# A fused attention and feed-forward kernel: weight operands formed earlier, combinations kept in PSUM, and activation sums moved to GpSimd

## The chip, the cores and the metric

One core of a Trainium2 chip runs the whole kernel in one launch. The metric is the device time of one execution in microseconds, a median over runs. Engine names are short: PE is TensorE, DVE is VectorE, ACT is ScalarE, POOL is GpSimd, SP is SyncE, which issues the DMAs.

## The reference

Three parts follow one another. The input of each is the output of the one before.

```python
def _attn_ref(q, k, v, w1, b1, w2):           # (4, 8, 576, 64)
    scores = scale * np.matmul(q, k.transpose(0, 1, 3, 2))
    ...
    scores = scores + bias.transpose(2, 0, 1)[None, :, :, :]
    ...
def _moe_ref(x, w_in, w_out, a, b):           # 2304 tokens, 512 -> 2048 -> 512
    h = x @ w_in
    P = a[0] + a[1] * h + a[2] * h2 + a[3] * h3
    Q = 1.0 + np.abs(b[0]) * np.abs(h) + np.abs(b[1]) * h2
    g = P / (Q + 1e-06)
    return (g @ w_out).astype(np.float32)
def _moe2_ref(x, w1, w2, w3, w_out):          # 512 -> 768 -> 512
    h = np.maximum(np.maximum(x @ w1, x @ w2), x @ w3)
    return (h @ w_out).astype(np.float32)
```

## The kernel before

Float32 products are made from operands split in a high and a low part (type fp32r), with three matmuls for each product: high by high, high by low, low by high. So every operand needs a cast for its high part (ACT) and a subtraction for its low part (mostly POOL). The weights arrive as 64-bit numbers; a shift on ACT (L605), another on DVE (L606) and a join on DVE (L611) make 32-bit ones of them.

**Attention** fills the span to about 343 us, and **the feed-forward part** follows to about 760. It takes the tokens in five blocks (0 to 4) of 512, 512, 256, 512 and 512. A block has sixteen steps, one for each 128 of the 2048 hidden columns. `ffn_tick(n)` writes one step: twelve matmuls for `ph` (the hidden columns of step n), twelve for `y` (the second matmul of step n-2), and between them the rational function g: `rat_poly`, `rat_inv`, `rat_newton` on ACT and DVE, and `rat_split`, whose high part is an ACT cast (L554) and whose low part is POOL's `gs` (L555). Each `g` tile comes from a ring of pools ("big").

**The third part (moe2)** runs from about 757 to the end. It works on three super blocks of 768 tokens (`sbk` 0 to 2). In each there are nine units `un` = 3 jp + w, where w is one of the three weight matrices and jp one of three pairs of 128-column groups. A unit is a two by two block product made with seven products instead of eight (Strassen's method in Winograd's form). `product` is six matmuls of 384 columns into one PSUM bank `pr`; `combine` adds the seven into the four results; `result` takes the maximum over w into `m`. The combination `c` goes to SBUF (L763) and the maximum L766 runs one or two products later, kept in a list by `after`. With w = 2 the finished `m` is split into `h2` (L753 on ACT, L751 on POOL). The steps of the w_out matmul (`o`, L828), two after each product, fill the next jp.

Seven products need seven weight operands (four sums of blocks among them) and seven activation operands (again with four sums). Before the change the 64-bit weights of moe2 are made 32-bit in blocks 1 and 3 and written to memory (`mn_d`, `mon_d`). They are read back in the last block and in super block 0 by `operand_stages`, one unit after the other: load, four sums on DVE (L643 to L646), casts on ACT (L655), low parts on POOL (L662), and a store to `ms_d` (L663). Super blocks 1 and 2 load the finished parts from `ms_d` (L689). The activation sums are four DVE operations of 768 columns (L718 to L721), with casts on ACT (L709) and low parts on POOL (L710, L711), in steps 9 to 15 of block 4 and, for the later super blocks, from product (7, 0) to (8, 6) of the super block before (`YN`).

PSUM has two `wide` tiles of two banks and four single banks. The `o` sums use both wide tiles and two of the four banks while they run, so that a product then has two banks left, and the bank of product n is written again by product n+2.

The order on SP, PE, DVE and POOL is that of the program text (`MANF`); ACT runs in program order too. `moe_product` sets the order in moe2: the matmuls, `combine`, the `o` steps, the delayed work of `product_tick`, and then one or two stages of the weight queue (`op_next`) and one of the y queue.

## Time and profile before

| | us |
|---|---|
| runs | 1055.9, 1059.98, 1060.53 |
| median of the three | 1059.98 |
| profiled execution, device time | 1058.46 |
| profiled execution, span | 1056.7 |
| PE busy in the span | 1009.1 |
| DVE, ACT, POOL busy | 786.5, 633.2, 478.8 |

Times in the trace count from the start of the span. An engine's busy time over a stretch is what its instructions cover; the rows further down give it by stretch, and PE's granted clock beside it (1.00 is 2.4 GHz, half of it 1.2 GHz). In the timeline a bracket such as [0.90 <-POOL gs L555] is the idle time of the engine ahead of the row, and what ended it. The PE rows overlap slightly, since matmuls are pipelined.

### The profile page before, as it was taken

What the parts mean: (1) busy time and instruction counts of PE and PEld (TensorE: products, weight loads), DVE (VectorE), ACT (ScalarE), POOL (GpSimd) and SP (SyncE); (2) the same over time, 40 slices, a digit from 0 to 9 for tenths busy, and PEclk for the clock granted to TensorE, in tenths of its full rate; (3) what the DMA queues carried; (4) which work ended last, traced back from release to release, by engine and by line L of the source; (5) the groups of instructions that cost most, each with busy time, mean ns of one, the idle gap of its engine ahead of it and who ended that gap; (6) DMA issues with size and microseconds to landing.
All of it is one profiled execution on the core that took longest, in us unless ns stands there. A gap on an engine that the chain in (4) does not pass through costs nothing. (4 is left out here: it accounts for less than half of the span.)

```text
span 1056.7 us, 17453 instructions
## 1 busy us (share of the span) xinstructions
PE 1009.1 (96%) x6050; PEld 824.1 (78%) x6050; DVE 786.5 (74%) x1549; ACT 633.2 (60%) x1258; POOL 478.8 (45%) x634
## 2 busy tenths in 40 slices
PE   6899999999998999999999999999899999999997
PEld 2368777777776678788899888788798989988996
DVE  8876587877675789889888899888797655565543
ACT  8867676777677778777778777778542121131111
POOL 4035677768686345422324223338677351152111
PEclk9999999999999999999999999999999999999999
DMA  7977666565544143044420344243186548744711
GB/s 256 333 249 210 235 217 197 174 207 194 172 143 148 54 145 100 1 150 130 149 80 2 100 140 150 100 165 114 69 310 254 195 148 283 246 160 161 270 49 60
DMA packets 69127, 172.22 MB, mean 163 GB/s; under 512 B 7088, under 2 KB 22960, under 8 KB 69040
## 3 DMA queue, kind: packets, MB, share of 16 engines
q1 hardware_dynamic: 69040, 171.12, 48.3%
q8 instruction: 47, 0.77, 0.3%
q14 instruction: 40, 0.33, 0.1%
HBM read 118.27 MB, written 52.82 MB: 162 GB/s over the span
## 5 line engine op out<-in xcount | busy, mean ns | idle before, releaser
L779 PE MATMUL pr<-yo,ws 128*128 128x384 f32 x945 | 221.9, 339 | 8.6 <-DVE m L760 5.2
L507 PE MATMUL y<-gs,wwo 128*128 128x512 f32 (+1 forms) x940 | 215.0, 375 | 5.1 <-POOL gs L555 4.1
L507 PE MATMUL ph<-xs,wwi 128*128 128x512 f32 (+1 forms) x930 | 207.0, 370 | 1.6 <-POOL xs L499 1.4
L555 POOL TENSOR_TENSOR gs<-g,gs 128x512 fp32r<-128x512 f32 (+1 forms) x80 | 95.5, 1193 | 226.8 <-ACT gs L554 156.4
L507 PEld LDWEIGHTS y<-gs,wwo 128*128 128x128 f32 x940 | 165.0, 189 | 41.9 <-POOL gs L555 7.0
L779 PEld LDWEIGHTS pr<-yo,ws 128*128 128x128 f32 x945 | 172.6, 189 | 23.0 <-DVE m L760 6.3
L507 PEld LDWEIGHTS ph<-xs,wwi 128*128 128x128 f32 x930 | 162.2, 188 | 35.4 <-POOL xs L499 3.6
L266 ACT ACTIVATE e<-e,st 128x576 f32<-128x576 f32 x144 | 110.8, 771 | 69.1 <-DVE st L260 46.5
L260 DVE CUSTOM_DVE_ANT_0 e<-s,bias 128x576 f32<-128x576 f32 x144 | 103.6, 752 | 17.4 <-PE s L235 11.1
L828 PE MATMUL o<-wmo,h 128*128 128x512 f32 x324 | 100.1, 397 | 2.8 <-DVE ot L813 2.0
L794 ACT COPY u<-pr 128x384 f32<-128x384 f32 x27 | 13.0, 481 | 146.0 <-PE pr L779 96.0
L751 POOL TENSOR_TENSOR h<-m,h 128x384 fp32r<-128x384 f32 x36 | 36.7, 1040 | 134.7 <-ACT h L753 109.8
L528 ACT ACTIVATE s<-ph,keep 128x512 f32<-128x512 f32 (+1 forms) x80 | 49.3, 617 | 64.2 <-PE ph L507 64.0
L235 PE MATMUL s<-k,qs 128*128 128x288 f32 x512 | 85.0, 308 | 1.9 <-ACT bo L197 1.0
L307 PEld LDWEIGHTS tp<-ident,e 128*128 128x128 f32 x564 | 60.4, 141 | 32.1 <-issue 15.9
L349 PE MATMUL av<-at,v 128*64 128x320 f32 (+3 forms) x576 | 77.4, 393 | 7.2 <-ACT at L1030 5.6
L307 PE MATMUL tp<-ident,e 128*128 128x128 f32 x564 | 78.6, 280 | 0.6 <-DVE att L328 0.6
L235 PEld LDWEIGHTS s<-k,qs 128*128 128x128 f32 x512 | 70.8, 190 | 4.1 <-DVE st L260 1.9
L530 DVE SCALAR_TENSOR_TENSOR g<-g,keep,s 128x512 f32<-128x512 f32 (+1 forms) x80 | 55.3, 691 | 21.6 <-ACT g L529 20.2
L542 DVE SCALAR_TENSOR_TENSOR g<-g,keep,s 128x512 f32<-128x512 f32 (+1 forms) x80 | 55.5, 694 | 16.8 <-ACT s L536 12.0
L828 PEld LDWEIGHTS o<-wmo,h 128*128 128x128 f32 x324 | 58.7, 189 | 6.7 <-DVE ot L813 2.1
L779 PE MATMUL pr<-yl,ws 128*128 128x384 f32 x189 | 63.4, 335 | 0.0
(140 smaller groups left out, 1842.0 us busy)
## 6 DMA issues: line engine op xcount, KB each, us to landing
ws<-ms_d SPq DMA_DIRECT2D x54, 512.0 KB, 4.1
ms_d<-ws SPq DMA_DIRECT2D x27, 512.0 KB, 3.1
bias_d<-bo SPq DMA_DIRECT2D x36, 288.0 KB, 6.6
kr<-in_k SPq DMA_DIRECT2D x16, 576.0 KB, 3.9
qr<-in_q SPq DMA_DIRECT2D x16, 576.0 KB, 4.9
bias<-bias_d SPq DMA_DIRECT2D x16, 576.0 KB, 5.8
nr<-in_m SPq DMA_DIRECT2D x18, 512.0 KB, 3.6
wrwin<-in_wi SPq DMA_DIRECT2D x16, 512.0 KB, 4.7
```

What stands on the lines that cost most here:

```text
L235: pe.matmul(pt[:, x, :HS], lhsT=qs[:, u, t * P:(t + 1) * P], rhs=ks[u][:, w, x * HS:(x + 1) * HS], start=w == 0, stop=w == 1,)
L260: dve.tensor_tensor_reduce(out=dst, in0=src, in1=bs, op0=ALU.add, op1=ALU.min, scale=-0.125, scalar=3.0e38, accum_out=st[:, u:u + 1],)
L266: act.activation(et[:, u], et[:, u], AF.Exp, bias=st[:, u:u + 1], scale=-1.0, accum_out=st[:, 2 + u:3 + u])
L307: pe.transpose(tp[:, j * P:(j + 1) * P], flat[:, 640 * u + j * P:640 * u + (j + 1) * P], ident)
L349: pe.matmul(po[r, :n], lhsT=l, rhs=m, start=j == 0, stop=j == 4, skip_group_check=True)
L507: pe.matmul(po, lhsT=wpart(key, a, k), rhs=rhs, start=first and i == 0, stop=last and i == 2)
L528: act.activation(s, ph, AF.Abs, scale=B0)
L530: dve.scalar_tensor_tensor(q, q, B1, s, ALU.mult, ALU.add)
L542: dve.scalar_tensor_tensor(u, u, A0, s, ALU.add, ALU.mult)
L555: pool.tensor_tensor(t[1], u, f32(t[0]), ALU.subtract)
L779: pe.matmul(pt, lhsT=w[:, a, ch * P:ch * P + P], rhs=ys[c][ch], start=ch == 0 and i == 0, stop=ch == 1 and i == 2,)
L828: pe.matmul(po, lhsT=h[:, a, (tt % 3) * P:(tt % 3 + 1) * P], rhs=mo_t[j][:, c], start=j == 0 and i == 0, stop=j == NF2 - 1 and i == 2,)
```

## The change

- **Weight units.** The round trip through `mn_d` and `mon_d` is gone. `unit_stages` loads two raw 64-bit pieces, makes them 32-bit, forms the four sums on POOL, and splits all parts; a table `PLAN` says which unit is made in which block and at which steps. Units 2, 3, 4 are made in block 1, unit 5 in block 2, units 6, 7, 8 in block 3, units 0 and 1 in block 4. The last two stay in SBUF. The others pass through one tile with two halves (`wring`) to `ms_d`, and super block 0 loads them back like the later super blocks do; the first three of these loads stand in steps 13 to 15 of block 4 (`WPN`).
- **w_out tiles.** `out_stages` makes the six tiles 32-bit and splits them during the first products of super block 0, one stage after each product.
- **g tiles.** All but the first three use two halves of one tile (`gring`).
- **Activation sums.** They stand on POOL, in another form of the same products (t3, t2, t1, t4), in steps 5 to 12 of block 4 and from product (6, 2) to (8, 5).
- **Combinations.** `result` writes the combination back into the PSUM bank and takes the maximum from there at once. The delayed list and the `c` tiles go. The low part of `h2` is issued with its cast.
- **Last unit.** The last `o` steps are set up at product 20 (`OE`); the order of PE's instructions at the end is the same.

```diff
-KN = {... 'YL': 7, 'YS': 9, ... 'OPA': 2, 'OPR': 2, 'WR': 7, ... 'YN': [(7, 0), (7, 3), (7, 6), (8, 3), (8, 4), (8, 5), (8, 6)], ...}
+KN = {... 'YL': 4, ... 'YN': [(6, 2), (6, 4), (6, 6), (7, 1), (7, 3), (7, 5), (8, 1), (8, 3), (8, 4), (8, 5)], ... 'YSN': {5: 2, 6: 2, 7: 1, 8: 1, 9: 1, 10: 1, 11: 1, 12: 1}, 'PLAN': [(2, 1, [0, 2, 3, 4, 5, 6, 7, 8]), (3, 1, [4, 6, 7, 8, 9, 10, 11, 12]), ... (5, 2, [1, 3, 5, 6, 8, 10, 12, 14]), ... (0, 4, [0, 2, 3, 4, 5, 6, 7, 8]), (1, 4, [6, 8, 9, 10, 11, 12, 13, 14])], 'WPN': {13: 1, 14: 1, 15: 1}, ...}
...
+            bt = gring[0][:, len(gring) % 2]
+            gring.append(None)
...
-            sp.dma_start(dst, f32(t))
-
-        return [load, rebias, join]
...
         def sums():
-            r = box["r"]
-            box["s"] = t = raw(f"os{un}", [P, 2, 512], F32)
...
-            seng.tensor_tensor(s1, a21, a22, ALU.add)
-            seng.tensor_tensor(s3, a11, a21, ALU.subtract)
...
+            pool.tensor_tensor(s1, a21, a22, ALU.add)
+            pool.tensor_tensor(s3, a11, a21, ALU.subtract)
+            pool.tensor_tensor(s2, s1, a11, ALU.subtract)
+            pool.tensor_tensor(s4, a12, s2, ALU.subtract)
...
+                t = wring[0][:, g % 2, :, :n]
+            box[g] = t
             act.copy(t[:, 0], source(g))
...
+            lambda: (ld0(), ld1()), lambda: (re0(), jo0()), lambda: (re1(), jo1()), lambda: (sums(), hi(0)),
+            lambda: (lo(0), hi(1)), lambda: (lo(1), hi(2)), lambda: (lo(2), hi(3)), lambda: lo(3),
...
+        return [load, rebias, lambda: (join(), hi()), lo]
...
     def y_stages(sbk):
         b11, b12, b21, b22 = (yr[sbk, h, t] for h in range(2) for t in range(2))
-        tt = (dve if KN["YD"] else pool).tensor_tensor
+        tt = pool.tensor_tensor
...
+        def t3():
+            tt(b12, b22, b12, ALU.subtract)
+
+        def t2():
+            for i, x in enumerate(pieces("t2")):
+                tt(x, b12[:, i], b11[:, i], ALU.add)
...
-    def result(sbk, un, jj, th, a_, b_, op, lag):
+    def result(sbk, un, jj, th, pt, a_, b_, op):
...
-        c_ = sb.tile([P, 512], F32, tag="xs", name=f"c{sbk}_{un}_{jj}{th}", bufs=KN['NXS'])[:, :TH]
-        dve.tensor_tensor(c_, a_, b_, op)
-
-        def more():
-            dve.tensor_tensor(m, m, c_, ALU.max)
-            if w == 2:
-                after(1, lambda: h2_make(sbk, 2 * jp + jj, th))
-
-        after(lag, more)
+        dve.tensor_tensor(pt, a_, b_, op)
+        dve.tensor_tensor(m, m, pt, ALU.max)
+        if w == 2:
+            h2_make(sbk, 2 * jp + jj, th)
...
+        for st in plan.pop((n // NF, n % NF), []):
+            st()
...
         if sbk == 0:
-            for _ in range(2 if n in (0, 3) else 1):
-                op_next()
+            op_next()
```

Where instructions now stand shows at three places. First DVE, in super block 0 between unit 2 and unit 3 (`pr0_2_4` is the bank of super block 0, unit 2, product 4; `os` are weight sums, `nno` a w_out tile). Before:

```order
L763 TENSOR_TENSOR c0_2_01_8893<-pr0_2_2_8886,u40_2_8878 128x384
L766 TENSOR_TENSOR m0_0_8597<-m0_0_8597,c0_2_10_8864 128x384
L766 TENSOR_TENSOR m0_0_8597<-m0_0_8597,c0_2_11_8880 128x384
L766 TENSOR_TENSOR m0_0_8597<-m0_0_8597,c0_2_01_8893 128x384
L643 TENSOR_TENSOR os6_8912<-or6_8797 128x256
L644 TENSOR_TENSOR os6_8912<-or6_8797 128x256
L645 TENSOR_TENSOR os6_8912<-os6_8912,or6_8797 128x256
L646 TENSOR_TENSOR os6_8912<-or6_8797,os6_8912 128x256
L760 TENSOR_TENSOR m0_3_8905<-pr0_3_1_8919,u10_3_8906 128x384
```

And now, on the same engine at the same place:

```order
L782 TENSOR_TENSOR pr0_2_4_8817<-pr0_2_4_8817,u30_2_8797 128x384
L783 TENSOR_TENSOR m0_0_8558<-m0_0_8558,pr0_2_4_8817 128x384
L615 SCALAR_TENSOR_TENSOR nno4_8831<-nro4_8747 128x512
L782 TENSOR_TENSOR pr0_2_2_8835<-pr0_2_2_8835,u40_2_8824 128x384
L783 TENSOR_TENSOR m0_0_8558<-m0_0_8558,pr0_2_2_8835 128x384
L610 TENSOR_SCALAR nro5_8799<-nro5_8799 128x512
L780 TENSOR_TENSOR m0_3_8857<-pr0_3_1_8862,u10_3_8858 128x384
```

Three maxima and four sums stood ahead of the `m` of unit 3; one shift of a w_out tile stands there now, and each maximum follows its combination.

Second DVE again, in the last unit (8) of super block 0, at the passage to super block 1 (`yr` are the activations, `u` partial results). Before:

```order
L800 TENSOR_TENSOR u30_8_9463<-pr0_8_6_9454,u20_8_9449 128x384
L721 TENSOR_TENSOR yr1_01_9239<-yr1_11_9243,yr1_00_9237 128x768
L763 TENSOR_TENSOR c0_8_10_9484<-u30_8_9463,pr0_8_3_9475 128x384
L804 TENSOR_TENSOR u40_8_9500<-pr0_8_4_9493,u20_8_9449 128x384
L763 TENSOR_TENSOR c0_8_11_9502<-pr0_8_4_9493,u30_8_9463 128x384
L763 TENSOR_TENSOR c0_8_01_9519<-pr0_8_2_9510,u40_8_9500 128x384
L766 TENSOR_TENSOR m0_6_9230<-m0_6_9230,c0_8_10_9484 128x384
L766 TENSOR_TENSOR m0_6_9230<-m0_6_9230,c0_8_11_9502 128x384
L766 TENSOR_TENSOR m0_6_9230<-m0_6_9230,c0_8_01_9519 128x384
L760 TENSOR_TENSOR m1_0_9537<-pr1_0_1_9544,u11_0_9538 128x384
```

And now:

```order
L815 TENSOR_TENSOR u30_8_9374<-pr0_8_6_9365,u20_8_9361 128x384
L782 TENSOR_TENSOR pr0_8_3_9382<-u30_8_9374,pr0_8_3_9382 128x384
L783 TENSOR_TENSOR m0_6_9132<-m0_6_9132,pr0_8_3_9382 128x384
L819 TENSOR_TENSOR u40_8_9410<-pr0_8_4_9403,u20_8_9361 128x384
L782 TENSOR_TENSOR pr0_8_4_9403<-pr0_8_4_9403,u30_8_9374 128x384
L783 TENSOR_TENSOR m0_6_9132<-m0_6_9132,pr0_8_4_9403 128x384
L782 TENSOR_TENSOR pr0_8_2_9424<-pr0_8_2_9424,u40_8_9410 128x384
L783 TENSOR_TENSOR m0_6_9132<-m0_6_9132,pr0_8_2_9424 128x384
L780 TENSOR_TENSOR m1_0_9448<-pr1_0_1_9451,u11_0_9449 128x384
```

The y sum L721 is gone from DVE, and the three maxima have moved up to their combinations.

Third POOL, at steps 5 and 6 of block 4 (`gs4_1_1` is the low part of hidden group 1 in block 4, `wg` a kept weight part, `yo` and `yl` low parts of the activations). Before:

```order
L555 TENSOR_TENSOR gs4_1_1_8040<-g4_1_7986,gs4_1_0_8039 128x512
L662 TENSOR_TENSOR ws0_0_1_8006<-os0_7909,ws0_0_1_8006 128x512
L662 TENSOR_TENSOR ws0_0_2_8052<-or0_7907,ws0_0_2_8052 128x256
L555 TENSOR_TENSOR gs4_2_1_8090<-g4_2_8034,gs4_2_0_8089 128x512
L662 TENSOR_TENSOR ws0_0_3_8056<-os0_7909,ws0_0_3_8056 128x512
L555 TENSOR_TENSOR gs4_3_1_8147<-g4_3_8084,gs4_3_0_8146 128x512
```

And now:

```order
L562 TENSOR_TENSOR gs4_1_1_8018<-gring_4861,gs4_1_0_8017 128x512
L729 TENSOR_TENSOR yr0_01_7933<-yr0_11_7937,yr0_01_7933 128x768
L733 TENSOR_TENSOR yt_8029<-yr0_01_7933,yr0_00_7931 128x384 x2
L655 TENSOR_TENSOR wg0_0_7985<-nn0_0_7884,wg0_0_7985 128x512
L562 TENSOR_TENSOR gs4_2_1_8067<-gring_4861,gs4_2_0_8066 128x512
L737 TENSOR_TENSOR yt_8029<-yr0_11_7937,yt_8029 128x384 x2
L708 TENSOR_TENSOR yo0_0_8079<-yr0_00_7931,yo0_0_8079 128x384
L709 TENSOR_TENSOR yl0_0_8080<-yr0_00_7931,yo0_0_8079 128x384
L655 TENSOR_TENSOR wg0_1_8034<-ns0_7980,wg0_1_8034 128x512
L562 TENSOR_TENSOR gs4_3_1_8123<-gring_4861,gs4_3_0_8122 128x512
```

Between two `gs` there now stand four instructions, with the activation sums among them, where one or two low parts stood.

## Rows read from the trace of the kernel before

**Rows 1.** The page, busy time (share of the span) and instructions of each engine.

```profile
PE 1009.1 (96%) x6050; PEld 824.1 (78%) x6050; DVE 786.5 (74%) x1549; ACT 633.2 (60%) x1258; POOL 478.8 (45%) x634
```

**Rows 2.** Stretches: length, busy PE, PEld, DVE, ACT, POOL, clock, DMA share, GB/s.

```profile
437.00:526.00 89.00, 88.74 (x385) 71.72 (x384) 77.79 (x120) 65.45 (x115) 24.67 (x21) 1.00 0.37 120
526.00:575.00 49.00, 48.49 (x384) 47.13 (x383) 43.24 (x99) 39.42 (x102) 16.71 (x20) 1.00 0.18 58
663.00:741.00 78.00, 77.61 (x335) 62.35 (x334) 65.82 (x98) 59.91 (x102) 41.11 (x35) 1.00 0.36 125
741.00:760.00 19.00, 16.35 (x62) 12.26 (x61) 15.34 (x23) 12.31 (x21) 13.07 (x12) 0.92 0.07 28
780.00:800.00 20.00, 16.08 (x83) 15.32 (x82) 19.02 (x29) 6.37 (x13) 16.30 (x13) 0.91 0.71 259
840.00:860.00 20.00, 17.67 (x93) 16.20 (x92) 13.54 (x20) 5.93 (x10) 13.34 (x13) 1.00 0.43 132
940.00:960.00 20.00, 17.67 (x94) 16.17 (x93) 12.55 (x19) 5.92 (x10) 13.37 (x12) 1.00 0.38 122
```

**Rows 3.** Timeline at 746 to 757: start, duration, instruction, [idle before <-releaser].

```profile
746.78 2.90 PE L507 MATMUL ph<-xs,wwi 128*128 128x512 f32 x12
...
750.99 2.83 PE L507 MATMUL y<-gs,wwo 128*128 128x512 f32 x11 [0.90 <-POOL gs L555]
...
756.07 2.16 PE L507 MATMUL y<-gs,wwo 128*128 128x512 f32 x6 [1.26 <-POOL gs L555]
```

**Rows 4.** Timeline at 786 to 795, DVE and PE, super block 0.

```profile
786.43 3.41 DVE L766 TENSOR_TENSOR m<-m,c 128x384 f32<-128x384 f32 x3
...
793.30 1.10 DVE L646 TENSOR_TENSOR os<-or,os 128x256 f32<-128x256 f32 x1
...
794.92 0.69 PE L779 MATMUL pr<-yo,ws 128*128 128x384 f32 x1 [3.92 <-DVE m L760]
```

**Rows 5.** Timeline at 849 to 858, passage from super block 0 to 1.

```profile
849.30 1.75 DVE L721 TENSOR_TENSOR yr<-yr,yr 128x768 f32<-128x768 f32 x1 [2.33 <-POOL yl L711]
...
851.56 0.97 PE L779 MATMUL pr<-yo,ws 128*128 128x384 f32 x4 [1.68 <-DVE c L763]
...
857.37 0.79 PE L779 MATMUL pr<-yo,ws 128*128 128x384 f32 x3 [0.65 <-DVE m L760]
```

**Rows 6.** Timeline at 1037 to 1043, the last unit with two banks.

```profile
1037.79 0.87 PE L779 MATMUL pr<-yo,ws 128*128 128x384 f32 x4
...
1039.04 0.56 DVE L804 TENSOR_TENSOR u<-pr,u 128x384 f32<-128x384 f32 x1 [0.96 <-PE pr L779]
...
1039.31 0.87 PE L779 MATMUL pr<-yo,ws 128*128 128x384 f32 x4
...
1039.52 0.55 DVE L763 TENSOR_TENSOR c<-pr,u 128x384 f32<-128x384 f32 x1
...
1042.24 0.73 PE L828 MATMUL o<-wmo,h 128*128 128x512 f32 x2 [0.33 <-ACT h L753]
```

**Rows 7.** Groups by line and shape: count | busy us, mean ns | idle before, releasers.

```profile
L555 POOL TENSOR_TENSOR gs<-g,gs 128x512 fp32r<-128x512 f32 x64 | 83.6, 1307 | 196.7 <-ACT gs L554 130.8 <-issue 55.2 <-PE y L507 8.3
...
L766 DVE TENSOR_TENSOR m<-m,c 128x384 f32<-128x384 f32 x72 | 46.0, 676 | 0.0
...
L402 DVE SCALAR_TENSOR_TENSOR wnwin<-wrwin 128x512 int32<-128x512 int32 x16 | 17.2, 1074 | 0.1
L611 DVE SCALAR_TENSOR_TENSOR nn<-nr 128x512 int32<-128x512 int32 x18 | 12.4, 687 | 0.8
L555 POOL TENSOR_TENSOR gs<-g,gs 128x256 fp32r<-128x256 f32 x16 | 11.9, 741 | 30.1 <-ACT gs L554 25.6 <-issue 4.2 <-POOL xs L499 0.3
L655 ACT CAST ws<-os 128x512 fp32r<-128x512 f32 x18 | 11.2, 620 | 3.6 <-DVE os L645 2.8 <-DVE os L646 0.8
...
L643 DVE TENSOR_TENSOR os<-or 128x256 f32<-128x256 f32 x9 | 7.7, 860 | 0.0
```

**Rows 8.** The page, DMA issues: count, KB each, us to landing.

```profile
ms_d<-ws SPq DMA_DIRECT2D x27, 512.0 KB, 3.1
```

More of the change, by code (lines that the diff above doesn't have):

```diff
@@ L510, in tile_attention_moe @@
     gt, ph_t, bun = {}, {}, {}
+    gring, wring = [], []
     def ffn_h(blk, f):
@@ L524, in rat_poly @@
         s = bank(f"s{blk}_{f}")[:, :n]
-        bt = (slot if blk == 0 and f < KN["RS"] else big)(f"g{blk}_{f}", [P, 2, 512], F32)
+        if blk == 0 and f < KN["RS"]:
+            bt = slot(f"g{blk}_{f}", [P, 2, 512], F32)
+        else:
+            if not gring:
+                gring.append(big("gring", [P, 2, 2, 512]))
+            bt = gring[0][:, len(gring) % 2]
+            gring.append(None)
         q, u = bt[:, 0, :n], bt[:, 1, :n]
@@ L652, in hi @@
         def hi(g):
             n = 256 * len(PAIR[g])
-            t = slot(f"ws0_{un}_{g}", [P, 2, n], F32R)
+            if keep:
+                t = slot(f"wg{un}_{g}", [P, 2, n], F32R)
+            else:
+                if not wring:
+                    wring.append(big("wring", [P, 2, 2, 512], F32R))
+                t = wring[0][:, g % 2, :, :n]
+            box[g] = t
             act.copy(t[:, 0], source(g))
-            for i, pr in enumerate(PAIR[g]):
-                ws[0, un, pr] = t[:, :, 256 * i:256 * i + 256]
@@ L708, in y_operand @@
         last = yo[sbk, "low"][:, n % 3]
-        act.copy(t[:, :2], src)
-        pool.tensor_tensor(t[:, 2], src[:, 0], f32(t[:, 0]), ALU.subtract)
-        pool.tensor_tensor(last, src[:, 1], f32(t[:, 1]), ALU.subtract)
+        if isinstance(src, list):
+            for i in range(2):
+                act.copy(t[:, i], src[i])
+        else:
+            act.copy(t[:, :2], src)
+            src = [src[:, 0], src[:, 1]]
+        pool.tensor_tensor(t[:, 2], src[0], f32(t[:, 0]), ALU.subtract)
+        pool.tensor_tensor(last, src[1], f32(t[:, 1]), ALU.subtract)
         yo[sbk, pr] = (t[:, 0], t[:, 1]), (t[:, 2], last)
@@ L735, in product_tick @@
         clock[0] += 1
-    wq = [(sbk, un, g) for sbk in range(1, NSB) for un in range(3 * NJP) for g in range(4)]
+    kept = [un for un, blk, _ in KN["PLAN"] if blk == len(blocks) - 1]
+    wq = [(sbk, un, g) for sbk in range(NSB) for un in range(3 * NJP) if sbk or un not in kept for g in range(4)]
     def operands_next():
@@ L927, in tile_attention_moe @@
     ystq = []
[L928 to L941 removed]
+    ost = [out_stages(j) for j in range(NF2)]
+    opq = [ost[0][0]]
+    for j, st in enumerate(ost):
+        opq += [s_[0] for s_ in ost[j + 1:j + 2]] + st[1:]
     def op_next():
@@ L1096, in moe_product @@
         pt = product(sbk, un, pr)
[L1097 removed]
+        if n in (1, 3, 4, 6):
             operands_next()
@@ L1101, in moe_product @@
             osteps[0] = o_steps(sbk if jp else sbk - 1, jp - 1 if jp else NJP - 1)
-        for _ in range(KN["OR"]):
+        end = (sbk, un) == (NSB - 1, 3 * NJP - 1)
+        for _ in range(KN["OE"][n] if end else KN["OR"]):
             next(osteps[0], None)
@@ L1129, in tile_attention_moe @@
             moe_product(*m)
-        assert not opq and not wq
+        assert not opq and not wq and not plan
         for _ in range(2):
             product_tick()
-        for _ in o_steps(NSB - 1, NJP - 1):
+        for _ in osteps[0]:
             product_tick()
```

142 lines of the change are left out of this document (63 added, 79 removed).

## The prediction, made before the changed kernel ran

> **What bounds the kernel now.** I read the busy line of the page first: TensorE (PE) is busy 1009.1 of the 1056.7 us span and nothing else comes near [rows 1]. So the only gain within reach is PE time that is idle or run at the half clock, and I looked for it with the table of stretches [rows 2]. The two stretches inside the feed-forward blocks have PE busy 88.74 of 89 and 48.49 of 49 us at clock 1.00: nothing to win there, only to lose. The last block up to 741 is as full (77.61 of 78). Four places are not full. The end of the feed-forward part, 741 to 760, has 16.35 of 19 busy and a mean clock of 0.92. The stretch 780 to 800 has 16.08 of 20 at 0.91. The stretches 840 to 860 and 940 to 960 have 17.67 of 20 each.
>
> The timeline then names the cause of each. **End of the feed-forward part** [rows 3]: PE runs one block of twelve `ph` matmuls (2.90 us), then waits 0.90 us for the GpSimd (POOL) half of `gs` and, one block of twelve on, 1.26 for POOL again. With a shorter wait between them, for ACT's half, these make the 2.65 us that are idle there. **At 790** [rows 4]: VectorE (DVE) does three `m` maxima out of SBUF in 3.41 us and four weight sums, the last taking 1.10, and only then the `m` of L760 that frees a PSUM bank; PE waits 3.92 us for it. **At the super-block boundaries** [rows 5]: the y sum L721 waits 2.33 us for POOL and takes 1.75 ahead of the `c` of L763, for which PE waits 1.68; then PE waits 0.65 for the `m` of L760, which again stands behind three maxima. Together 2.33 us, which is the idle time of that stretch.
>
> **What the change removes.** At 790 no sums are left in moe2, and the maxima no longer come as a batch in front of L760. I count the 3.92 us of waiting in full, and 1.6 for the clock: a mean of 0.91 over 20 us is 3.6 us at half level, worth 1.8 if PE worked throughout; part of that is inside the wait. 5.5 us. At each boundary the y sum has left DVE and the maxima are spread, so 2.33 goes, twice: 4.7. At the end of the feed-forward part the y splits and the weight splits are gone from POOL behind the last `gs`, so I let two of the three waits go (2.65 less one of 1.26, because with no `ph` block left to cover it the last chain must still be waited for: 1.4) and the clock loss, 0.08 of 19, 1.5. 2.9 us. At the tail the `h` wait of 0.33 goes [rows 6], since `h2_make` no longer waits a product: 0.3. **Gains 13.4.** Bounds: 9 if only the stall at 790 and half of the rest go; 18 if the slower first matmuls behind each wait come back too (one alone took 0.97 for four where 0.87 is usual [rows 5, 6], and at half clock it is more).
>
> **What it adds in the feed-forward blocks.** PE is full there, so the question is whether `gs` comes late. Per step of 5.56 us (89/16) POOL had one `gs` of 1.307 [rows 7] and 196.7/64 = 3.07 us of idle time ahead of it, two thirds of that for ACT's half of `gs`. The change gives blocks 1 and 3 three weight units each, in place of half of the narrow work. Per unit: four POOL sums of 128x256 at 0.74 (the 256 wide `gs` [rows 7]) = 2.96, four low parts, three at 1.3 and one at 0.74 = 4.6; ACT two shifts and four casts at about 0.62 (L655 [rows 7]), one of them narrower; DVE two joins at 0.69 (L611) and two shifts, which I put at no more than the joins. In blocks 1 and 3 twelve narrowings each go and six come, so DVE gets lighter by six joins and six shifts (at most 8 us), ACT heavier by some 3, POOL by 3 x 7.6 = 23: from 24.67 to 47 us of 89, or 53%. The last block already has POOL at 41.11 of 78 (53%) with PE at 77.61 [rows 2], so that share alone is no loss. The sharp steps are those with sums: 1.31 + 2.96 + 1.29 = 5.56, the whole step. A late `gs` costs nothing until it uses up the `ph` block that stands between: 2.90 less the 1.26 that a `gs` is waited for without one [rows 3], about 1.6 us.
>
> The last block is the fullest. Its steps 5 and 6 carry the y sums, priced from the two `gs` forms (0.566 us for each 256 columns: 1.87 for 768, 1.02 for 384). Step 5: 1.31 + 1.87 + 2 x 1.02 + 1.29 = 6.5; step 6: 1.31 + 4 x 1.02 + 1.29 = 6.7. Against 5.56 POOL falls 0.9 and then 2.1 late; 2.1 less 1.6 is half a microsecond of PE. The short block 2 is tight on other engines: DVE 43.24 and ACT 39.42 of 49 [rows 2], to which unit 5 adds 2 x 0.69 and two shifts (about 2.4), and 2 x 0.62 + 3 x 0.62 + 0.4 = 3.5. That still fits (45.7 and 42.9), but unevenly: 0.8 us, from 0 to 3.
>
> There is one new wait. Each hi cast of units 2 to 8 writes a half of `wring` that the store of two parts before must have read. The low part ends 2 x 1.3 us after ACT's `gs` cast, the store takes 3.1 to land [rows 8], 5.7 in all, and the cast comes one step of 5.56 plus about 2 us of ACT work later. About 1.8 us of slack, gone when POOL is late by more (the sums steps) or the store slower. Behind a waiting cast on ACT stands the next step's |h|; ACT has a quarter of each step free (65.45 of 89 [rows 2]), so I price it 0.4, from 0 to 4. DVE joins that run beside POOL can take 1.074 instead of 0.687 (L402 beside L611 [rows 7]): 18 x 0.39 = 7 us of DVE over 350, hidden by DVE's 11 us free in each 89. **Feed-forward costs: 0.5 + 0.8 + 0.4 + 0.3 for the rest = 2.0, from 0 to 9.**
>
> The Trainium skill (SBUF — State Buffer, section "Who interferes with whom") says more on such pairs: a DVE instruction with two SBUF inputs and a GpSimd instruction that reads SBUF shut each other out for a whole instruction. By that a join could wait out one POOL sum or low part, up to 1.3 us by the `gs` row; 18 joins would then cost DVE 23 us, not 7, and since DVE's free time in these blocks still covers it, the sum would gain perhaps 1 us. The row that agrees is the three maxima at 3.41 against 3 x 0.676 (L766 mean [rows 4, 7]).
>
> **What it adds in moe2.** The write-back lengthens the chain that frees a bank. Where two banks are left, product n+2 takes the bank of product n. In the tail a product starts at 1037.79 and the next at 1039.31: period 1.52, deadline 3.04. DVE's `u` starts 1.25 behind the product's start, the next operation 0.48 later [rows 6]. Now u4, the combination and the dependent maximum stand before the release: 1.25 + 0.48 + 0.55 + 0.55 = 2.83, so 0.2 to spare. It just fits; what disturbs DVE there (an `ot` copy in front) costs PE. Such copies fall beside product 4 in a few units: 0.8 us, from 0 to 2 while the chain fits (beyond that see the second rival). In units 1 and 2 of the first super block no w_out work stretches the period (a product is 1.52 less two matmuls at 2.90/12, 1.04, so 7.3 us a unit) while the six w_out tiles are joined on DVE: 9 operations of 0.55 plus two to three joins and shifts make 6.5 to 7.5 of 7.3 us. Four banks cover bursts; 0.7 us, from 0 to 3. The 28 reloads run where 259 GB/s at a DMA share of 0.71 was seen [rows 2], in place of stores and loads of about the same size, and each is issued two units ahead; 0.3, from 0 to 2. The combinations themselves cost nothing: DVE does as many, at 0.55 with a PSUM input [rows 6] against a mean of 0.676 without [rows 7]. **moe2 costs 1.8, from 0 to 7.**
>
> **Sum.** -13.4 + 2.0 + 1.8 = -9.6 on the profiled execution of 1058.46 us: 1048.9. The median shown, 1059.98, is 1.5 higher than that execution and the runs spread over 4.6, so I do not add the difference in full: **1049 us**.
>
> **Rivals.**
> First, slower: POOL becomes the bound of the feed-forward steps. If GpSimd's 128x256 sums or low parts cost more than the `gs` rows say, or stores hold the casts, the lateness in the sums step and the one behind it passes 1.6 us, and PE waits as it does at 756, 1.26 each [rows 3]. Nine units by two steps is 18 x 1.26 = 22.7 in place of the 2.0: 1058.46 - 13.4 + 1.8 + 22.7 = 1069.6. It decides where the four sums take over 4.6 us instead of 2.96 (5.56 + 1.6 less `gs` and a low part). Against it: the last block before at POOL 53%. For it: the sums L643 on the much faster DVE took 0.860 beside POOL [rows 7].
>
> The Trainium skill (GPSIMD Engine Reference, section "4.1 Engine selection") sends elementwise work to VectorE and puts GpSimd at about half its speed for two inputs. By that rule moving the sums is the wrong way; it is this rival's ground, and the 0.741 of the 256 wide `gs` already holds that lower speed.
>
> Second, no change: the write-back does not fit. If the dependent maximum waits longer for the combination than a plain 0.55 (the trace of before has no such pair through PSUM), each product 4 in the 16 units with w_out work and a second pass through the bank stalls by the excess. At 0.5 us, 16 x 0.5 = 8: 1057. It decides at 0.2 us more per chain.
>
> Third, a smaller gain: the joins and reloads leave the stall at 790 standing elsewhere. 5.5 of the gain is lost: 1054.4, at the edge.
>
> **How the numbers follow.** Forecast, 1043 to 1053: 0.60. Third rival, 1053 to 1055: 0.10, split over the bound. Second: 0.14. First: 0.16, of which a quarter stops short of +0.5%. What this kernel's measurement can tell from no change is 0.5%, 5.3 us: faster is below 1054.7, slower above 1065.3. Faster 0.60 + 0.07 = 0.67; slower 0.12; same 0.21. The range takes in the full gains with no costs (1058.46 - 18 = 1040) and reaches over the second rival to 1062; outside lie most of the first rival and 0.04 below.
>
> **What would show it.** Right: 780 to 800 and both boundaries read PE busy over 19.5 of 20 at clock 1.00; one `gs` wait is left near the end of the feed-forward part; PE in the blocks stays within 0.5 us of full. Wrong: `gs` waits in the steps with sums (first rival), `pr` waits for the maximum in every unit (second), ACT waits for stores at the hi casts.

## The result and the profile after

The changed kernel takes 1046.7 us, the median of four runs from 1045.53 to 1047.1. The kernel before, on the same chip, took 1058.25, so the ratio is 0.9889, with an interval of 0.9861 to 0.9917. The forecast was 1049. The profiled execution of the changed kernel took 1045.53 us with a span of 1043.7, which is 13.0 less than the span of before.

Part of any such difference has nothing to do with the change. The first feed-forward matmul starts at 343.53 us in the trace of before, at 343.75 in that of after, and between 340.3 and 345.3 in the other kernels here, though nothing that was changed runs before it. So traces are compared below from that matmul to the end of the span: 1056.7 - 343.53 = 713.17 us before, 1043.7 - 343.75 = 699.95 after. The change is worth **13.2 us** by that measure, which the rest of this document calls the rest time. Each rest time comes from one execution of its kernel, so a difference of a few tenths between two kernels is not shown to be more than chance.

The stretches of the kernel after, with the columns of [rows 2]:

```profile
437.00:526.00 89.00, 88.71 (x385) 71.68 (x384) 72.92 (x111) 67.84 (x120) 44.52 (x42) 1.00 0.27 95
526.00:575.00 49.00, 47.96 (x372) 46.01 (x371) 43.12 (x98) 41.83 (x105) 24.92 (x29) 1.00 0.30 108
663.00:741.00 78.00, 77.32 (x333) 61.78 (x332) 64.37 (x94) 62.07 (x108) 55.67 (x52) 1.00 0.30 102
741.00:760.00 19.00, 18.18 (x82) 14.80 (x81) 12.45 (x18) 11.91 (x22) 8.80 (x8) 1.00 0.64 222
760.00:780.00 20.00, 20.00 (x113) 19.45 (x112) 15.54 (x31) 6.96 (x13) 3.89 (x3) 1.00 0.80 299
780.00:800.00 20.00, 20.00 (x110) 19.06 (x109) 14.28 (x27) 5.44 (x11) 7.86 (x7) 1.00 0.87 324
840.00:860.00 20.00, 20.00 (x109) 18.90 (x108) 10.42 (x19) 4.53 (x9) 9.76 (x11) 1.00 0.51 178
940.00:960.00 20.00, 19.21 (x102) 17.77 (x101) 10.46 (x19) 1.55 (x3) 2.37 (x3) 1.00 0.52 183
```

The two places that lost most are full: 780 to 800 has PE busy 20.00 of 20 where it had 16.08, at clock 1.00 where it had 0.91 [rows 2]. The end of the feed-forward part goes from 16.35 to 18.18 of 19 and keeps the full clock. POOL's load in the blocks is what was worked out (44.52 us in the block of 437 to 526, 47 forecast), and PE stays full beside it. The two stretches that lose are block 2, 47.96 after 48.49, and the last block, 77.32 after 77.61; what they cost in time is more, and is counted further down.

What is left stands in the timeline, shown here at the end of the feed-forward part (first two rows, an earlier and the last wait for `gs`), and then at the passage to super block 1:

```profile
735.07 2.13 PE L507 MATMUL y<-gs,wwo 128*128 128x512 f32 x8 [0.38 <-POOL gs L562]
...
755.56 2.82 PE L507 MATMUL y<-gs,wwo 128*128 128x512 f32 x11 [0.82 <-POOL gs L562]
```

```profile
862.20 0.56 DVE L819 TENSOR_TENSOR u<-pr,u 128x384 f32<-128x384 f32 x1 [0.37 <-PE pr L794]
...
862.67 0.56 DVE L782 TENSOR_TENSOR pr<-pr,u 128x384 f32<-128x384 f32 x1
...
863.26 0.55 DVE L783 TENSOR_TENSOR m<-m,pr 128x384 f32<-128x384 f32 x1
...
863.74 0.68 DVE L828 COPY ot<-o 128x512 f32<-128x512 f32 x1
...
864.47 0.73 PE L843 MATMUL o<-wmo,h 128*128 128x512 f32 x2 [0.79 <-DVE ot L828]
```

One `gs` wait of 0.82 remains of the 2.65 us. At the passage no product waits: the chain of a product 4 (L819, L782, L783) runs as worked out, and its product starts at 860.94, so the bank is free 863.26 + 0.55 - 860.94 = 2.87 us on, against a deadline of 3.04. What waits is a w_out matmul, for the copy of an `ot` tile that DVE reaches only after that chain. The kernel before has this wait too, but shorter:

```profile
873.83 0.74 PE L828 MATMUL o<-wmo,h 128*128 128x512 f32 x2 [0.19 <-DVE ot L813]
```

The groups by line show how the prices held: the maximum from PSUM, one of the four sums on GpSimd, a join on DVE, and a hi cast with its wait for the store:

```profile
L783 DVE TENSOR_TENSOR m<-m,pr 128x384 f32<-128x384 f32 x72 | 39.9, 554 | 2.5
...
L615 DVE SCALAR_TENSOR_TENSOR nn<-nr 128x512 int32<-128x512 int32 x18 | 13.7, 763 | 1.8
...
L631 POOL TENSOR_TENSOR ns<-nn 128x256 f32<-128x256 f32 x9 | 6.7, 744 | 0.0
...
L648 ACT CAST wring<-nn 128x256 fp32r<-128x256 f32 x7 | 2.8, 400 | 1.2 <-DMA ms_d<-wring 1.2
```

A maximum costs 0.554 us where the one out of SBUF cost 0.676 [rows 7], and there are no more cases of three in 3.4 us. A sum on POOL costs 0.744, as taken. The casts waited 1.2 us in all for stores, on ACT, in two places (522 and 660), and PE has no wait behind them that it does not have in the kernel before.

### The profile page after: what moved, and what is told of

It reads as the page before. It is cut to its first block, busy times and chain, and to the rows that moved or that the text cites. A ratio compares the mean times of both kernels' runs of the same rounds, so it can differ in the third digit from the quotient of the medians.

```text
span 1043.7 us, 17477 instructions
## 1 busy us (share of the span) xinstructions
PE 1002.6 (96%) x6050; PEld 819.3 (78%) x6050; DVE 752.8 (72%) x1501; ACT 635.0 (61%) x1264; POOL 518.2 (50%) x691
## 5 line engine op out<-in xcount | busy, mean ns | idle before, releaser
L794 PE MATMUL pr<-yo,ws 128*128 128x384 f32 x875 | 205.9, 338 | 0.1
L562 POOL TENSOR_TENSOR gs<-gring,gs 128x512 fp32r<-128x512 f32 (+1 forms) x77 | 91.2, 1185 | 160.3 <-ACT gs L561 83.2
L794 PEld LDWEIGHTS pr<-yo,ws 128*128 128x128 f32 x875 | 159.0, 188 | 13.2 <-DVE m L783 0.7
L537 DVE SCALAR_TENSOR_TENSOR gring<-gring,keep,s 128x512 f32<-128x512 f32 (+1 forms) x77 | 53.0, 689 | 31.4 <-ACT gring L536 30.7
L549 DVE SCALAR_TENSOR_TENSOR gring<-gring,keep,s 128x512 f32<-128x512 f32 (+1 forms) x77 | 53.2, 691 | 16.3 <-ACT s L543 12.3
L191 PE MATMUL pb<-h,keep 128*32 128x288 f32 x576 | 48.2, 442 | 16.8 <-ACT bo L197 8.8
```

Of the source, the lines that this page charges most:

```text
L537: dve.scalar_tensor_tensor(q, q, B1, s, ALU.mult, ALU.add)
L549: dve.scalar_tensor_tensor(u, u, A0, s, ALU.add, ALU.mult)
L562: pool.tensor_tensor(t[1], u, f32(t[0]), ALU.subtract)
L794: pe.matmul(pt, lhsT=w[:, a, ch * P:ch * P + P], rhs=ys[c][ch], start=ch == 0 and i == 0, stop=ch == 1 and i == 2,)
```

## The experiments

My theory was that each of the four places had its own cause, so that no one part of the change brings the gain, and that POOL has room in the feed-forward blocks up to about 1.6 us of lateness in a step. The rivals were that one part does it all (the write-back, or the engine of the sums), and that the longer chain in PSUM or a full POOL eats the gain.

### One part alone: the write-back

The kernel before, with `result` and `h2_make` of the kernel after:

```diff
-        dve.tensor_tensor(c_, a_, b_, op)
-        def more():
-            dve.tensor_tensor(m, m, c_, ALU.max)
...
+        dve.tensor_tensor(pt, a_, b_, op)
+        dve.tensor_tensor(m, m, pt, ALU.max)
```

> The kernel before with one part of the change: the combination is written back into PSUM and the maximum taken from there at once, the h2 low part with its cast. Weight and activation sums stay on DVE where they were. My theory (each of the four places has its own cause): the 0.65 us waits at the two boundaries and the h waits at the tail go, and of the 3.92 us at 790 some 2 to 3, since the three maxima in 3.41 us no longer stand in a batch ahead of the four sums; the end of the feed-forward part stays (2.65 us idle), and so do the waits behind the y sum (1.68 each). About 5 us faster than before, 1053. Rival one (the write-back is the whole change): 10 us or more faster. Rival two (the longer chain does not fit two banks): no faster, waits of about 0.5 us at product 4 of most units.

Measured: 1050.77 us, ratio 0.9941 (0.9918 to 0.9965); rest time 706.5, so 6.6 us of the 13.2. The stretch at 741 stays as it was, the one at 780 mends in part:

```profile
741.00:760.00 19.00, 16.33 (x62) 12.31 (x62) 14.21 (x22) 12.31 (x21) 13.08 (x13) 0.91 0.11 46
...
780.00:800.00 20.00, 18.69 (x99) 16.89 (x98) 19.38 (x30) 8.98 (x18) 17.30 (x15) 1.00 0.68 246
```

The timeline there, DVE alone, shows what is left of the backlog: the sums still stand ahead of the `m` that frees the bank (L756 here).

```profile
789.28 0.95 DVE L645 TENSOR_TENSOR os<-os,or 128x256 f32<-128x256 f32 x1
...
790.26 1.12 DVE L646 TENSOR_TENSOR os<-or,os 128x256 f32<-128x256 f32 x1
...
791.30 0.55 DVE L756 TENSOR_TENSOR m<-pr,u 128x384 f32<-128x384 f32 x1
```

Of the 3.92 us that stretch had idle, 1.31 remain. The write-back alone is half of the gain, not the whole of it. At the passages it did more than I had expected: the wait of 1.68 us behind the y sum, which was to stay, fell to 0.40 and 0.45. It also has a price there: the wait of the w_out matmul for `ot` is 0.79 us in this kernel already, where it was 0.19.

### The other part alone: the sums on GpSimd

The kernel before, with its two switches for the engine of the sums turned:

```diff
-'SD': 1, 'YD': 1
+'SD': 0, 'YD': 0
```

> The kernel before with the weight sums and the activation sums on GpSimd in place of DVE, at the places in the program where they stood. My theory (GpSimd helps only because the work was also moved into the feed-forward blocks): at the end of the feed-forward part POOL has more to do behind the last gs, and the idle time of 2.65 us there grows to 4 to 6; at 790 the units wait for POOL (2.96 us of sums and 4.6 of low parts a unit of 7.3); the boundaries lose the DVE part of their wait. Net within 4 us of before. Rival (the engine of the sums is what counted): 8 us or more faster, with the stall at 790 gone.

Measured: 1057.13 us, ratio 0.9984 (0.9967 to 1.0001), which is not clear of no change; rest time 710.1, 3.1 us under the kernel before. Two rows of its timeline say why so little came of it:

```profile
750.14 2.13 PE L507 MATMUL y<-gs,wwo 128*128 128x512 f32 x8 [2.15 <-POOL gs L555]
...
798.67 0.74 PE L828 MATMUL o<-wmo,h 128*128 128x512 f32 x2 [3.14 <-POOL h L751]
```

At the end of the feed-forward part one wait for `gs` alone is 2.15 us now, and at 790 PE no longer waits for DVE but for POOL, which has 19.84 of 20 us busy there (780 to 800) and reaches the low part of `h` late. In these two places the engine is not the point: the sums had to leave the stretch altogether. At the passages the engine is enough. There the y sum no longer stands on DVE, and PE is busy 19.73 of 20 us instead of 17.67 [rows 2]:

```profile
840.00:860.00 20.00, 19.73 (x106) 18.43 (x105) 13.12 (x21) 6.58 (x11) 17.20 (x14) 1.00 0.52 178
```

### The maximum at once, but out of SBUF

The kernel after with the combination in SBUF again, in the ring of the `u` tiles:

```diff
-        dve.tensor_tensor(pt, a_, b_, op)
-        dve.tensor_tensor(m, m, pt, ALU.max)
+        c_ = sb.tile([P, 512], F32, tag="att", ...)[:, :TH]
+        dve.tensor_tensor(c_, a_, b_, op)
+        dve.tensor_tensor(m, m, c_, ALU.max)
```

> The changed kernel with the combination in SBUF again and the maximum taken from there at once (not delayed). The bank comes free one DVE operation earlier, 0.55 us, but the maximum reads SBUF twice: 0.676 mean instead of 0.554, and 1.1 where POOL runs. My theory: what counted was that no batch of maxima stands ahead of a bank's release; so the time stays within 2 us of the changed kernel, with L783 longer beside POOL. Rival (PSUM is what counted, by keeping the maximum off the port that POOL shares): 5 us or more slower than the changed kernel.

Measured: 1048.05 us, ratio 0.9911 (0.989 to 0.9931); rest time 703.0, 3.1 us over the kernel after. The maximum is the dearer one on average, and the reason is that some are long. The second and third row give the shortest, median and longest in ns, from PSUM in the kernel after and from SBUF here:

```profile
L784 DVE TENSOR_TENSOR m<-m,c 128x384 f32<-128x384 f32 x72 | 49.5, 687 | 2.5
...
L783 DVE TENSOR_TENSOR m<-m,pr x72: 553/554/556, 771.3 to 1029.6; 128x384 f32<-128x384 f32 x72
...
L784 DVE TENSOR_TENSOR m<-m,c x72: 557/558/1485, 771.3 to 1033.0; 128x384 f32<-128x384 f32 x72
```

Between the two theories: the ratio says 2.3 us, the traces 3.1, where I had expected at most 2 and the rival 5. The intervals of the two ratios overlap, so the size rests on the traces. Some 2 to 3 us of the write-back's worth is that the maximum reads PSUM; that the rest comes from taking it at once is inferred from the run with the write-back alone, not shown by a run of its own. The loss stands at 780 to 800 (1.6 us), where PE has 19.01 of 20 busy and the joins of the w_out tiles are, and at the passages (0.6 and 0.7 us). There a long maximum stands beside POOL's work; ACT casts `h` from it, and ACT's copy of `u`, for which PE waits, stands behind the cast:

```profile
845.31 1.31 DVE L784 TENSOR_TENSOR m<-m,c 128x384 f32<-128x384 f32 x1
...
848.95 0.96 PE L795 MATMUL pr<-yo,ws 128*128 128x384 f32 x4 [0.43 <-ACT u L810]
```

### The weight sums on DVE, at the new places

```diff
-            pool.tensor_tensor(s1, a21, a22, ALU.add)
+            dve.tensor_tensor(s1, a21, a22, ALU.add)
...
```

> The changed kernel with the weight sums on DVE, at the same steps of the feed-forward blocks. DVE gets 12 operations of 0.5 to 0.9 us in each of three blocks (8 us of its 16 free in 89), POOL loses 9 of its 45. My theory: neither engine bounds PE there, so the time stays within 1.5 us of the changed kernel; in block 2, where DVE has 43.1 of 49, it could lose 0.5 to 1. Rival by the rule that elementwise work belongs on VectorE: 3 us or more faster than the changed kernel, with the waits of 548 to 555 and 734 gone.

Measured: 1046.23 us, ratio 0.9895 (0.9873 to 0.9916); rest time 700.6, 0.6 us over the kernel after. The four sums are faster on DVE, 0.58 at most and 0.42 at best against 0.74 on POOL, and block 2 is what pays:

```profile
L634 DVE TENSOR_TENSOR ns<-nn,ns 128x256 f32<-128x256 f32 x9 | 5.2, 580 | 0.3
...
L633 DVE TENSOR_TENSOR ns<-ns,nn 128x256 f32<-128x256 f32 x9 | 3.7, 416 | 0.0
```

```profile
526.00:575.00 49.00, 47.35 (x356) 44.61 (x355) 43.27 (x98) 40.60 (x102) 20.44 (x23) 1.00 0.31 113
```

The time is the same. PE has 47.35 us busy in block 2 instead of 47.96, since a second wait for `gs`, of 0.48 us, has come at 560; against that the wait of 0.38 at 735 in the last block is gone, as the rival had it. The faster engine for one instruction is not the better place for it here.

### The activation sums on DVE, at the new places

```diff
-        tt = pool.tensor_tensor
+        tt = dve.tensor_tensor
```

> The changed kernel with the activation sums (t3, t2, t1, t4) on DVE, at the same places. My theory: with two banks left, each of them stands in front of a bank's release whose slack is 0.2 to 0.7 us; t3 (768 columns, 1.1 to 1.75 us) and the six of 384 columns cost 2 to 3 us at each of the two passages: 4 us slower than the changed kernel, from 2 to 6. Rival (spreading them was enough, DVE is half idle in that stretch): within 1 us.

Measured: 1049.28 us, ratio 0.9903 (0.9872 to 0.9935); rest time 703.5, 3.5 us over the kernel after. By the ratios alone the two kernels can't be told apart; by the rest time the size is what I had expected and the place is not. At the passages nothing is lost beyond 0.4 us each. The loss is in block 4:

```profile
700.00:741.00 41.00, 37.65 (x162) 29.83 (x161) 38.44 (x53) 32.66 (x57) 28.21 (x27) 1.00 0.19 71
```

```profile
718.43 2.45 DVE L741 TENSOR_TENSOR yr<-yt,yr 128x384 f32<-128x384 f32 x2
...
723.80 0.69 ACT L542 ACTIVATE s<-gring,keep 128x512 f32<-128x512 f32 x1 [3.76 <-DVE gring L537]
...
730.18 2.81 PE L507 MATMUL y<-gs,wwo 128*128 128x512 f32 x11 [0.97 <-POOL gs L562]
...
737.99 2.37 PE L507 MATMUL y<-gs,wwo 128*128 128x512 f32 x9 [1.99 <-POOL gs L562]
```

PE has 37.65 of these 41 us busy, against 40.62 in the kernel after. DVE carries six of the instructions that make g, and beside POOL two sums of 384 columns take 2.45 us (for the later super blocks the same line takes 0.55 each); the chain of g stands behind them, and ACT waits 3.76 us for it, where it waits 0.51 in the kernel after. POOL's `gs` ends that chain, and PE waits 0.97 and 1.99 us for it, where the kernel after has one wait of 0.38. So in the last block the sums belong on POOL, and at the passages their new places, one or two products apart, were enough for either engine. My theory of the passages fell.

### A longer chain on the bank

Each maximum from PSUM twice, with the same result:

```diff
         dve.tensor_tensor(m, m, pt, ALU.max)
+        dve.tensor_tensor(m, m, pt, ALU.max)
```

> The changed kernel with each maximum from PSUM taken twice (72 more DVE operations of 0.55 us, same result). It lengthens the chain that frees a bank. In the trace of the changed kernel the chain of a product 4 runs 1.26 + 0.47 + 0.59 + 0.55 = 2.87 us from the product's start, against a deadline of 3.04 with two banks. My theory: with 0.59 more it is 3.46, 0.42 over, in the 16 units with w_out work: 6.7 us; units 1 and 2 of the first super block, where DVE has most of a period to do, lose 1 or 2 us each. 8 us slower than the changed kernel, from 5 to 11, the waits at product 4 and ended by the second maximum. Rival (the bank's release is not what the slack hangs on, DVE being 50% busy there): within 2 us.

Measured: 1061.67 us, ratio 1.0024 (1.0006 to 1.0042), which is 14 us over the kernel after; rest time 716.4, 16.4 over. The table of waits (us in total, times, longest) names the second maximum. Its row counts the weight loads (PEld), which run ahead of the matmuls; of the matmuls themselves the same table has 14 waits of 6.1 us in all, and the rest of the loss is in the slower matmuls behind them:

```profile
PEld pr L795 <- DVE m L784: 22.0, 46, 1.5
```

```profile
850.68 0.55 DVE L783 TENSOR_TENSOR m<-m,pr 128x384 f32<-128x384 f32 x1
...
851.27 0.55 DVE L784 TENSOR_TENSOR m<-m,pr 128x384 f32<-128x384 f32 x1
...
851.88 0.96 PE L795 MATMUL pr<-yo,ws 128*128 128x384 f32 x4 [0.33 <-DVE m L784]
```

The direction and the place are right, the size was twice mine. I had counted one wait for each unit. The rows show another: the maximum of product 4 delays the two operations of product 2, which follow on DVE at once, and their bank is late too. The matmul at 851.88, product 1 of the next unit, waits for that bank (46 waits of weight loads, not 16). About 4 us of the loss fall in units 2 and 3 of the first super block, where I had put 1 or 2 for each of units 1 and 2. So the slack of the write-back is real and small: one more DVE operation in the chain costs the whole gain of the change.

### Twice the sums on POOL

```diff
+            for _ in range(2):
+                sums4()
```

> The changed kernel with the four weight sums of each unit done twice on GpSimd (36 more operations of 0.74 us, same result): 5.92 us in a step instead of 2.96. It puts the price of the slower rival to the test. My theory: POOL's step becomes 1.3 + 5.92 + 1.29 = 8.5 of 5.56 us, the next gs is 2.95 late, 1.6 of it is covered by a ph block, and PE waits 1.35 for each of nine units: 12 us slower than the changed kernel, from 6 to 16, as gs waits in the step behind the sums. Rival (POOL has enough idle time around it, 45 of 89 us busy): under 3 us.

Measured: 1064.81 us, ratio 1.0047 (1.0028 to 1.0065); 16.7 us over the kernel after, rest time 718.4, 18.5 over. That is more than the range of 6 to 16. In blocks 1 and 3 PE loses about 1.1 us at the sums of the second and third unit (at 494, 517, 638 and 662), near the 1.35 worked out, and nothing at the first. What I had too low is the rest. Block 2 loses more, since its steps are half as long:

```profile
554.49 0.75 POOL L636 TENSOR_TENSOR ns<-nn,ns 128x256 f32<-128x256 f32 x1
555.19 0.73 POOL L633 TENSOR_TENSOR ns<-nn 128x256 f32<-128x256 f32 x1
...
558.83 1.44 PE L507 MATMUL y<-gs,wwo 128*128 128x256 f32 x5 [3.34 <-POOL gs L562]
```

and the last block over 6 us (663 to 760: 89.21 busy of 97, against 95.50 in the kernel after), where the y work stands in the same steps as the sums; one wait for `gs`, at 750, is 4.89 us there. The slower rival's mechanism is real; its condition, sums of over 4.6 us, was not met by sums of 2.96.

### The order of the w_out tiles

The waits for `ot` have one thing in common: token tiles 0 and 1 (and 2 and 3) of the `o` sums are two banks of one `wide` tile, and the matmuls of tile 1 come right behind tile 0's last. At the end of the kernel after, where each tile has six matmuls, the waits stand ahead of the twelve of tiles 1 and 2 and of the eighteen of tiles 3 to 5, so ahead of tiles 1 and 3 and of no other:

```profile
1031.83 3.00 PE L843 MATMUL o<-wmo,h 128*128 128x512 f32 x12 [0.78 <-DVE ot L828]
...
1035.70 4.32 PE L843 MATMUL o<-wmo,h 128*128 128x512 f32 x18 [0.88 <-DVE ot L828]
```

```diff
-        for tt in range(6):
+        for tt in (0, 2, 1, 3, 4, 5):
```

> The changed kernel with the six token tiles of the w_out steps in the order 0, 2, 1, 3, 4, 5. In the changed kernel's trace PE waits for the copy of an ot tile at 864.47 and 957 (about 1.05 us each, with the slower first matmul) and at the tail twice (1.05 and 1.1): tile 1 shares a two-bank PSUM tile with tile 0, and its matmuls wait until the copy of tile 0 has read. My theory: with tile 2 between them the copy is done in time: 4 us faster than the changed kernel, from 3 to 4.5. Rival (the wait is for the DVE's queue, whatever the tile): under 1.5 us.

Measured: 1041.06 us, ratio 0.9828 (0.9798 to 0.9858); rest time 695.6, 4.3 us under the kernel after. At the end PE runs all 39 last matmuls without a wait:

```profile
1023.13 9.04 PE L843 MATMUL o<-wmo,h 128*128 128x512 f32 x39
```

and 860 to 950 is full, 90.00 of 90. The wait was for the tile, not for DVE's queue.

### The end of the feed-forward part

Three more versions of that kernel moved the first products of moe2 about the last two y steps, where in the kernel after none stands ahead of the first and three ahead of the second.

> The token order 0, 2, 1, 3, 4, 5 of the run before, and the first three moe2 products moved ahead of the last-but-one y matmuls. In the changed kernel PE waits 0.82 us there for POOL's gs (about 1.1 with the slower first matmul), since no ph block is left to cover it. My theory: three products (3.1 us) cover that chain, and the time from the first feed-forward matmul to the end falls from 695.6 us (token order alone) by 1.0, to 694.6. Rival (the products wait for their banks or operands at that point, so the wait only moves): no gain, or up to 1 us slower.

```diff
-            ffn_tick(NS + mx)
-            for _ in range(KN["MIXN"]):
+            for _ in range(0 if mx else KN["MIXN"]):
+                moe_product(*mprod.pop(0))
+            ffn_tick(NS + mx)
```

Measured: 1039.51 us, ratio 0.9834 (0.9808 to 0.986), rest time 695.57: no gain. The wait moved to the second step, where no product stands now:

```profile
759.55 2.82 PE L507 MATMUL y<-gs,wwo 128*128 128x512 f32 x11 [1.02 <-POOL gs L562]
```

> As the run with the token order and the products moved, and besides: the four sums of unit 5 (block 2, the short one) in two steps instead of one, and the sums of the two units of block 4 on DVE. My theory: the gs wait in block 2 (0.63 us, and some 0.3 around 548) and a quarter of a microsecond at 734 go: 1.0 us less than the run with the order and products alone. Rival (block 2 is short of ACT and DVE time, not of POOL's): no difference.

```diff
+            eng = dve if keep else pool
...
-            lambda: ... lambda: (sums(), hi(0)),
+            *([lambda: sums(0), lambda: (sums(1), hi(0))] if un == 5 else [lambda: (sums(), hi(0))]),
```

Measured: 1040.98 us, ratio 0.9837 (0.9811 to 0.9863), rest time 695.57: no gain either. The wait at 734 did go, with the last units' sums on DVE, as it did in the run with all weight sums there. The wait at 555 in block 2 got shorter (0.20 us) and another came at 569 (0.38). What exactly runs out in that block, ACT, DVE or POOL, these runs don't tell.

> The token order, and two moe2 products ahead of each of the last two y steps (in the changed kernel: none ahead of the first, three ahead of the second). The run with three ahead of the first and none ahead of the second had the wait moved to the second (1.02 us). My theory: two products (2.1 us) cover the wait in each place, and the time from the first feed-forward matmul to the end falls from 695.6 to 694.6 us. Rival (the products' own work on ACT and DVE delays the chain that makes the last gs, so that a wait stays whatever the split): 695.2 or more.

```diff
-            ffn_tick(NS + mx)
-            for _ in range(KN["MIXN"]):
+            for _ in range(2):
                 moe_product(*mprod.pop(0))
+            ffn_tick(NS + mx)
```

Measured: 1038.94 us, ratio 0.9811 (0.976 to 0.9862), rest time 693.9, 1.7 us under the version with the token order alone and 6.0 under the kernel after. From 741 to the last unit PE has no idle time:

```profile
741.00:765.00 24.00, 24.00 (x113) 20.50 (x112) 16.15 (x25) 14.24 (x25) 9.63 (x8) 1.00 0.59 210
765.00:860.00 95.00, 95.00 (x514) 90.74 (x514) 58.36 (x110) 21.84 (x40) 40.35 (x38) 1.00 0.70 245
860.00:950.00 90.00, 90.00 (x480) 85.09 (x479) 47.82 (x88) 17.36 (x33) 33.52 (x33) 1.00 0.62 215
```

This is the fastest kernel of the study. By the ratios it can't be told from the other two with the token order; by the rest time it is 1.6 us ahead of them.

## Why the prediction was right, step by step

**Matmul by matmul.** The two kernels run the same matmuls in the same order. So one matmul's start in both traces, less the 0.22 us by which the first feed-forward matmul starts later, says how far the change has come by then. The last column is what the prediction added for the step above.

| matmul | before | after | moved, us | step | forecast |
|---|---|---|---|---|---|
| `y`, start of the last block | 666.32 | 667.82 | +1.28 | +1.3 | feed-forward blocks |
| `y` at the wait in that block | 732.77 | 735.07 | +2.08 | +0.8 | together +2.0 |
| first product of moe2 | 760.15 | 758.22 | -2.15 | -4.2 | -2.9 |
| product behind the stall at 790 | 797.87 | 790.44 | -7.65 | -5.5 | -5.5 |
| product, first passage | 857.37 | 847.44 | -10.15 | -2.5 | -2.33 |
| `o` behind it | 873.83 | 864.47 | -9.58 | +0.6 | moe2, together +1.8 |
| product, second passage | 952.17 | 940.05 | -12.34 | -2.8 | -2.33 |
| `o` behind it | 968.63 | 957.07 | -11.78 | +0.6 | |
| `o` at the tail | 1044.72 | 1031.83 | -13.11 | -1.3 | -0.3 |

**The four places.** All four gave at least what was claimed, for the cause that was named. At 790 the 5.5 us went in full, waiting and clock. At the end of the feed-forward part 2.65 us of idle time became 0.82, where I had left 1.26, and the clock stayed at 1.00: 4.2 us for 2.9, the rest being the slower matmuls behind the waits. At each passage somewhat more than the 2.33 went [rows 5]. At the tail no `h` wait is left; I had claimed the 0.33 of [rows 6] alone, and a second one of 0.47 behind it went too, with the slower matmuls behind both. The runs with one part each say that neither part is the whole: by the rest time 6.6 us for the write-back, 3.1 for the engine of the sums where they stood (by its ratio not clear of nothing), 13.2 for the change.

**The costs in the feed-forward blocks** were put at 2.0 and are 2.1. Block 2 has 1.1 of it, lost from 548 to its wait at 555 (0.8 forecast), and the last block 0.8 (0.5 forecast). So the sign that PE would stay within 0.5 us of full in the blocks was missed in block 2, which is 1.04 from it, and just missed in the last block (0.68). The busy time of the stretches shows only 0.53 and 0.29, because a matmul behind a wait is slower and counts as busy throughout. The casts' wait for stores was 1.2 us of ACT and none of PE (0.4 forecast). The lateness of 1.6 us that a `ph` block covers held: sums of 2.96 us passed in blocks 1 and 3 without a new wait, and sums of 5.92 cost 1.1 us at four of the six units there.

**The joins beside POOL.** In block work they took 0.763 on average against 0.687 before, 18 x 0.08 = 1.4 us of DVE; in blocks 1 and 3 PE has no new wait from it, and for block 2 that is not shown. The Trainium skill (SBUF — State Buffer, section "Who interferes with whom") says that such a pair contends and that this contention is an exclusive lock. The 1.375 us for each of two sums on DVE beside POOL in block 4 (L737, in the run with the activation sums on DVE), against 0.55 without it, agree; for the joins the rule's worst case, 23 us, was a bound that the program's order came nowhere near.

**The costs in moe2** were put at 1.8 and are 1.1, and here the step was wrong in its mechanism; that the size is near is luck. I had `ot` copies delay the bank of product 4. The products wait for nothing; it is the w_out matmuls that wait 0.79 us at each passage, for a tile that they share with the copy, where they waited 0.19 before. At the tail that wait is as long in the kernel before (0.78 and 0.87) as in the kernel after (0.78 and 0.88), so it is not new in kind. It is also why the stretch 940 to 960 reads 19.21, under the 19.5 that was set as a sign; in the first passage the wait lies just behind the stretch. Reordering the tiles took all of it away. The terms for units 1 and 2 (0.7) and for the reloads (0.3) came to nothing: 760 to 800 is full, at 299 and 324 GB/s.

**The second rival** (the write-back does not fit) was closer than its 0.14 says. The chain was worked out at 2.83 and is 2.87 us of 3.04. The longer chain turned the whole change into 1.0024 of before, because the delay is handed on to the next product on DVE, which the rival's price of 0.5 us for each unit left out.

**The first rival** had the right mechanism and a condition that wasn't met. The rule behind it, in the Trainium skill (GPSIMD Engine Reference, section "4.1 Engine selection"), that elementwise work goes to VectorE, with GpSimd at about half the speed for two inputs, is borne out for one instruction: 0.74 us against 0.42 to 0.58. It gives the wrong placement here: with the weight sums on DVE the time is the same, and with the activation sums on DVE it is 3.5 us longer by the rest time. DVE carries six instructions of the chain that PE waits for, and POOL only the last, `gs`; so work on DVE delays the chain at once, and work on POOL only where it is still running when `gs` is due.

**The sum** came out 3.5 us high: -9.6 was forecast for the profiled execution, and the table has -13.1. The costs make little of that, 3.2 us (2.1 and 1.1) for 3.8. The gains are 16.3 for 13.4. The term that was too small is for the most part the slower matmuls behind each wait, which go with the wait: the prediction named them in its upper bound of 18 and left them out of the sum. Beside them it counted one of two `h` waits at the tail and left too much of the last `gs` wait. What stays open is what runs out in block 2.

## What to carry to other kernels

Where one engine is full, read its few idle places by stretch and name for each the instruction that ended the wait and what stood ahead of that instruction in its queue; a backlog is mended by moving work out of the stretch, and changing its engine there helps only where the other engine has room, as at the passages, and moves the wait where it has not, as at 790. Where two kernels run the same matmuls in the same order, compare the starts matmul by matmul: busy time hides the slower matmuls behind a wait. Before making a chain longer that frees a buffer, count it against the number of periods the buffer lasts, and count the operations behind it on the same engine too: 0.17 us were to spare here, and one more operation cost 14 us. A tile of two banks is waited for as one, so the order of its users is worth a look: a permutation of six gave 4.3 us.
